# Top-k attention and a gated MLP on one core: the order of a pair of slots, and the merge of two sorted lists

## The chip, the cores and the metric

The kernel runs on one core of a Trainium2 chip. The time is device time in microseconds (us) of one execution. The kernel before has a median of 1507.23 us over 3 runs (1506.77 to 1514.11). Lines L1 and on are lines of the kernel before; PE is TensorE's matrix product, PEld its load of stationary weights, DVE VectorE, ACT ScalarE, POOL GpSimd, SP the engine whose queue issues nearly all DMAs.

## The reference

```python
# q, k, v: (8, 8, 576, 64); w_in: (512, 2048); w_out: (2048, 512); all float32
scores = scale * np.matmul(q, k.transpose(0, 1, 3, 2))
kth = np.partition(scores, -32, axis=-1)[..., -32:-31]
scores = np.where(scores >= kth, scores, -1000000000.0)
attn = np.exp(scores - np.max(scores, axis=-1, keepdims=True))
attn = attn / (np.sum(attn, axis=-1, keepdims=True) + 1e-09)
x = np.matmul(attn, v)              # heads put side by side: (4608, 512)
h = x @ w_in
g = h * (1.0 / (1.0 + np.exp(-1.702 * h)))
out = g @ w_out
```

Each row of scores has 576 entries; the 32 largest are kept, the rest get no weight. The attention's result is the input of a two-layer MLP with a sigmoid gate.

## The kernel before, in words

**Slots.** The attention is cut into 144 slots, 18 per batch. A slot is 128 query rows of one pair of heads (or 64 + 64 rows of two pairs of heads, for the ends of the rows). For a slot n the steps are: `scores` (PE, L282, into PSUM), `copy_scores` (ACT, L294, to the tile `sc` in SBUF), the search for the 32nd largest value (DVE), `bounds` (POOL, L368, two tiny instructions), `exponentials` (ACT: two Prelu, L388, and two Exp with their sums, L391), `split` (ACT, L462: the 16-bit halves of each word are put apart, then a DMA L464 writes them to memory as `rows`), `turn_by_dma` (SP, L470: a transposing DMA brings them back as `pt`), `values` (PE, L530), and the product with the inverse sums, which gives a piece of x (`x_of`, POOL, L544). The inverse sums are made by `invert` (DVE L421 and L423, then a widening copy on POOL, L425) and turned by PE (`sum_rows`, L519).

**The search.** From slot 12 on, the 576 scores of a row are halved: DVE takes the larger of each of 288 pairs (`greater`, L323), POOL makes the smaller ones with two integer instructions (the sum, L326, then the sum less the greater, L327; `lesser`). DVE then finds the 32 largest of `greater` with four rounds of MAX8 (L337) and three of MATCH_REPLACE8 (L340), and the 16 largest of `lesser` with two and one. The lists are sorted. `merge` (L344, one TENSOR_TENSOR with a reversed second input) takes the larger of the k-th of one and the (17-k)-th of the other, and `bound` (L347) reduces these to the cut. `find(n)` issues all of that for slot n, and in its middle `pair_up(n + 1)`.

**The MLP.** Work on 128 tokens is cut into four units. A unit is `hidden` (PE, L580, 32 matmul instructions), `tanh` (ACT, L597 and a copy L600), `gate` (POOL, L609 and L610) and `project` (PE, L628, 8 instructions). Lists in the program (`ready`, `to_gate`, `gated`, `to_project`) hand the units on; a step whose list is empty is left out. When a tile of tokens is done, `leave` (ACT, L634) and a DMA (L636) write it out.

**q and k.** From batch 1 on they are fetched by `load_both` (six DMAs on SP, L184 and L187, into one buffer), then `prepare_by_dma` puts halves apart (ACT, L240, tile `halves`), writes them (SP, L244 to L249) and leaves a transposing DMA (L253) for the list `turns`. FETCH and READY (L657 to L661) say how many slots before a batch each of its four pairs of heads is fetched and prepared; READY's offsets are even, so that `prepare_by_dma` falls into the first half of a pair of slots.

**The order.** It is written out by hand: each engine and each DMA queue runs its instructions in the order in which the program issues them. Slots 0 to 11 run singly (`slot`), with another search and transpositions on PE; they also round the weights. From slot 12 on `two_slots(n)` runs a pair of slots, n even (L842 to L921). On PE a pair before is: hidden, projection, row sums, scores n+2, values n-3 and n-2, scores n+3, hidden, projection. `last_slot` works off the MLP units left over at the end.

**Buffers that matter.** Scores of a slot fill four PSUM banks in two tiles (`ps_s`, 2 buffers), so scores of the next slot wait for the copy of the ones before. The hidden of the second half shares two PSUM buffers with the tile `o` of row sums and values. `pt` has 2 buffers, `sc` 4.

Of the kernel before, what the change touches and what calls it, by code (L numbers as in the profile page):

```python
# [9 lines left out]
ALU = mybir.AluOpType  # L10
ENG = mybir.EngineType
F32 = mybir.dt.float32
U32 = mybir.dt.uint32
I32 = mybir.dt.int32
# [4 lines left out]
P = 128  # L19
TOPK = 32  # L20
LOWEST = -3.4028234663852886e38
# [9 lines left out]
def kernel(  # L31
# [27 lines left out]
    nc = tc.nc  # L59
# [255 lines left out]

    greater, lesser = {}, {}

    def pair_up(n):

        sc = st[n]["sc"]  # L320
        a, b = sc[:, :, 0:HALF], sc[:, :, HALF:S]
        greater[n] = lefts.tile([P, 2, HALF], F32, name="greater", tag="left")
        nc.vector.tensor_tensor(out=greater[n][:], in0=a, in1=b, op=ALU.max)  # L323
        lesser[n] = raws.tile([P, 2, HALF], F32, name="lesser", tag="raw")
        whole = lesser[n][:].bitcast(I32)
        nc.gpsimd.tensor_tensor(out=whole, in0=a.bitcast(I32), in1=b.bitcast(I32), op=ALU.add)  # L326
        nc.gpsimd.tensor_tensor(out=whole, in0=whole, in1=greater[n][:].bitcast(I32), op=ALU.subtract)  # L327

    def topk_of_pairs(n):

        top = st[n]["top"] = small.tile([P, 2, TOPK + TOPK // 2], F32, name="top2", tag="top")
        cut = st[n]["cut"] = small.tile([P, 2], F32, name="cut")
        first, few = greater.pop(n), lesser.pop(n)
        left = lefts.tile([P, 2, HALF], F32, name="left2", tag="left")

        def largest(src, r, i):
            nc.vector.max(top[:, i, 8 * r : 8 * r + 8], src[:, i, :])  # L337

        def remove(to, src, r, i):
            nc.vector.match_replace(to[:, i, :], top[:, i, 8 * r : 8 * r + 8], src[:, i, :], LOWEST)  # L340

        def merge():
            rest = top[:, :, TOPK // 2 : TOPK]
            nc.vector.tensor_tensor(out=rest, in0=rest, in1=top[:, :, : TOPK - 1 : -1], op=ALU.max)  # L344

        def bound():
            nc.vector.tensor_reduce(  # L347
                out=cut[:], in_=top[:, :, TOPK // 2 - 1 : TOPK], axis=mybir.AxisListType.X, op=ALU.min, negate=True
            )

        ops = []
        for r in range(TOPK // 8):
            ops += [lambda r=r, i=i: largest(left if r else first, r, i) for i in range(2)]
            if r < TOPK // 8 - 1:
                ops += [lambda r=r, i=i: remove(left, left if r else first, r, i) for i in range(2)]
        ops += [lambda: pair_up(n + 1) if n + 1 < N else None]
        for r in range(TOPK // 8, TOPK * 3 // 16):
            ops += [lambda r=r, i=i: largest(few, r, i) for i in range(2)]
            if r == TOPK // 8:
                ops += [lambda r=r, i=i: remove(few, few, r, i) for i in range(2)]  # L360
        return ops + [merge, bound]

    def lows(n):

        top, cut = st[n]["top"], st[n]["cut"]
        low = st[n]["low"] = small.tile([P, 2], F32, name="low")
        for i in range(2):
            nc.gpsimd.tensor_scalar(  # L368
                low[:, i : i + 1], cut[:, i : i + 1], top[:, i, 0:1], -1.0, op0=ALU.add, op1=ALU.mult
            )  # L370

    def bounds(n):
# [23 lines left out]
    def divide(n):  # L396

        some = small.tile([P, 2], F32, name="some", tag="sums")
        nc.vector.tensor_scalar_add(some[:], st[n]["den"], 1e-9)
        rden = small.tile([P, 2], F32, name="rden", tag="inverse")  # L400
        nc.vector.reciprocal(rden[:], some[:])
        by = st[n]["by"] = xtt.tile([P, 2, P], F32, name="by", tag="xT_t")
        for i in range(2):
            nc.gpsimd.tensor_scalar(by[:, i, :], ident[:], rden[:, i : i + 1], None, op0=ALU.mult)

    sums = {}

    def sums_of(n):

        k = (n + 1) // 2  # L410
        if k not in sums:
            sums[k] = small.tile([P, 2, 2], F32, name="sums")
        return sums[k][:, (n + 1) % 2, :]

    def invert(n):

        k = (n + 1) // 2
        if k in sums:
            count = 2 if 2 * k < N else 1
            total = sums[k][:, 0:count, :]  # L420
            nc.vector.tensor_scalar_add(total, total, 1e-9)  # L421
            inverse = small.tile([P, 2 * count], F32, name="inverse")
            nc.vector.reciprocal(inverse[:], total.rearrange("p s j -> p (s j)"))  # L423
            wide = sums[k] = raws.tile([P, 2, 2, D], F32, name="wide", tag="raw")
            nc.gpsimd.tensor_copy(  # L425
                out=wide[:, 0:count, :, :].rearrange("p s j d -> p (s j) d"),
                in_=inverse[:].unsqueeze(2).to_broadcast([P, 2 * count, D]),
            )

    def turn(n, first, blocks):  # L430
        pr = st[n]["pr"]
# [84 lines left out]

    def sum_rows(m, to):

        nc.tensor.transpose(to, sums[(m + 1) // 2][:, (m + 1) % 2, :, :], ident[:])  # L519

    def values_at(m, o):

# [121 lines left out]
    def leave_all():  # L644
        while leaving:
            leaving.pop(0)()
# [8 lines left out]


    READY = (-12, -10, -4, -2)  # L657
    READY_1 = (-7, -4, -3, -2)
    FETCH = (-16, -11, -8, -3)
    FETCH_1 = (-12, -6, -3, -2)  # L660
    VALUES = (-1, 1, 1, 3)  # L661
    by_slot = dict(enumerate([2, 2, 3, 3, 3, 3, 3, 3, 3, 3, 2, 2]))
    for n in by_slot:
        first = sum(map(len, list(by_slot.values())[:n]))
# [87 lines left out]
    def bring_all():  # L752

        waiting = len(ready)
        while put_off:
            put_off.pop(0)()
        if len(ready) > waiting:
            hidden()
# [75 lines left out]
    def last_slot():  # L834
# [4 lines left out]
        if may_project(0):  # L839
            project()  # L840

    def two_slots(n):  # L842

        first, second = [later.pop(m, []) for m in (n, n + 1)]
        live = lambda m: 0 <= m < N
        aside = n < N

        def begin(todo):
            for fn, args in todo:
                if fn is not prepare_by_dma:  # L850
                    fn(*args)

        def prepare_some(todo):
            for fn, args in todo:
                if fn is prepare_by_dma:
                    fn(*args)

        def find(m):
            for i, op in enumerate(topk_of_pairs(m) if live(m) else [lambda: None] * 23):
                op()  # L860
                if i == 8 and m % 2 == 0:
                    invert(m - 2)
                if i > 1 and unfinished:
                    finish_one()

        def project_one():
            if may_project(0):
                project(True)

        def measure(m):  # L870
            if live(m):
                bounds(m)
            gate(aside)

        begin(first)
        measure(n - 1)
        if live(n - 1):
            exponentials(n - 1)
            split(n - 1)
        bring_all()  # L880
        find(n)
        hidden()
        project_one()
        tanh(aside)
        prepare_some(first)
        held = [m for m in (n - 3, n - 2) if live(m) and "rows" in st[m]]
        o = ps_t.tile([P, 2, 2, P], F32, name="o", tag="tp") if held else None
        for i, m in enumerate(held):
            sum_rows(m, o[:, i, 0, :])
        if live(n + 2):  # L890
            scores(n + 2)
            copy_scores(n + 2)
        leave_all()
        for i, m in enumerate(held):
            values_at(m, o[:, i, 1, :])
        if live(n - 1):
            turn_by_dma(n - 1)
        while turns:
            turns.pop(0)()
        if live(n + 3):  # L900
            scores(n + 3)
        begin(second)
        measure(n)
        if live(n):
            exponentials(n)
        if held:
            x = raws.tile([P, 2, 2, P], F32, name="x", tag="raw")
            nc.scalar.copy(out=x[:, 0 : len(held)], in_=o[:, 0 : len(held)])
            for i, m in enumerate(held):
                x_of(m, x[:, i, 1, :], x[:, i, 0, :])  # L910
        if live(n):
            split(n)
            turn_by_dma(n)
        hidden(ps_t)
        if live(n + 3):
            copy_scores(n + 3)
        tanh(aside)
        prepare_some(second)
        project_one()
        leave_all()  # L920
        find(n + 1)  # L921

    with tc.manual_schedule():
        opening()
        for n in range(SETTLED + 1):
            slot(n)
        pair_up(SETTLED + 1)
        for n in range(SETTLED + 1, N + 4, 2):
            two_slots(n)
        while ready or to_gate or gated or to_project:  # L930
            last_slot()
# [30 lines left out]
```

## Time and profile before

| what | value |
|---|---|
| median of the runs | 1507.23 us |
| the profiled execution's own time | 1512.53 us |
| its span in the profile | 1510.7 us |
| granted TensorE clock over the span | 0.983 |
| busy PE / PEld / DVE / ACT / POOL | 1443.9 / 1052.8 / 1378.1 / 1171.7 / 891.1 us |
| hidden L580 on PE | 489.6 us in 4096 recorded instructions |
| projection L628 on PE | 518.5 us in 1152 |
| merge L344 on DVE | 132 times, 484 ns mean |
| bound L347 on DVE | 132 times, 190 ns mean |
| `by` L404 on POOL | 22 times, 605 ns mean |
| transposition of pt, L470 | 133 issues, 4.7 us to landing (median) |
| transposition of q and k, L253 | 28 issues, 4.9 us to landing (median) |

The span is the profiled execution from its first to its last instruction. A line of the waits names who waited, for whom, and then the total in us, the number of times and the longest. A line of the timeline gives the start in us from the span's start, the duration, the engine, the line and the operation; consecutive instructions of one kind are merged (x8). Some matmul records are missing from a trace, so a hole in PE's line can be a missing record; L580 has 4608 instructions in the program.

### The profile page before, as it was taken

How to read it: one execution, taken by the hardware profiler on the slowest of the kernel's cores; microseconds unless marked ns; L12 is line 12 of the kernel's file. 1: busy time of each engine (PE TensorE's matmuls, PEld its weight loads, DVE VectorE, ACT ScalarE, POOL GpSimd, SP SyncE). 2: the span in 40 equal slices, each digit the busy share in tenths (PEclk: the TensorE clock that was granted, in tenths of full speed). 3: DMA queues.
4: the chain of work that ended last, by engine and by line, in shares of the span. 5: the costliest groups of instructions: out<-in, count | busy, mean ns of one | idle time of the engine just before them, and what ended most of it. 6: DMA issues, size and time to landing. Idle time of an engine off the chain costs nothing. (4 is left out here: it accounts for less than half of the span.)

```text
span 1510.7 us, 31439 instructions
## 1 busy us (share of the span) xinstructions
PE 1443.9 (96%) x10729; PEld 1052.8 (70%) x10729; DVE 1378.1 (91%) x4542; ACT 1171.7 (78%) x1846; POOL 891.1 (59%) x1117
## 2 busy tenths in 40 slices
PE   6789878999999999999999999999999999999998
PEld 5667555767777777767777767777777777777775
DVE  7999989999999999999999999999999999999800
ACT  6998878878878787888878787888878888777720
POOL 3788645666666666666666556666666666656500
PEclk7899989999999999999999999999999999999999
DMA  7451876766858587666767667585776767444520
GB/s 226 134 156 43 196 198 184 190 174 171 188 158 211 149 201 194 159 182 157 210 160 182 167 178 191 159 199 150 196 194 155 192 161 207 140 129 134 133 55 14
DMA packets 533777, 248.35 MB, mean 164 GB/s; under 512 B 465136, under 2 KB 507888, under 8 KB 533616
## 3 DMA queue, kind: packets, MB, share of 16 engines
q1 hardware_dynamic: 533184, 246.05, 62.1%
q8 instruction: 84, 1.38, 0.4%
q14 instruction: 77, 0.63, 0.1%
q10 hardware_dynamic: 432, 0.30, 0.1%
HBM read 45.09 MB, written 105.32 MB: 100 GB/s over the span
## 5 line engine op out<-in xcount | busy, mean ns | idle before, releaser
L580 PEld LDWEIGHTS ph<-xT,win 128*128 128x128 f32 x4096 | 474.3, 192 | 69.7 <-issue 53.7
L628 PE MATMUL po<-wout,th 128*128 128x512 f32 x1152 | 518.5, 593 | 1.5 <-POOL wout L147 1.5
L580 PE MATMUL ph<-xT,win 128*128 128x128 f32 x4096 | 489.6, 277 | 12.0 <-POOL xT L544 12.0
L628 PEld LDWEIGHTS po<-wout,th 128*128 128x128 f32 x1152 | 208.1, 191 | 211.1 <-issue 207.9
L337 DVE MAX8 top<-left 128x8 f32<-128x288 f32 x792 | 325.6, 446 | 0.0
L462 ACT COPY sc<-pr 128x2304 uint16<-128x2304 uint16 x133 | 281.5, 2117 | 2.2
L294 ACT ACTIVATE sc<-s_ps 128x576 f32<-128x576 f32 x288 | 172.0, 653 | 128.9 <-PE s_ps L282 126.7
L544 POOL TENSOR_TENSOR xT<-x 128x128 f32<-128x128 f32 x117 | 51.4, 457 | 332.4 <-DVE top L344 161.3
L340 DVE MATCH_REPLACE8 left<-top,left 128x288 f32<-128x288 f32 x528 | 229.7, 443 | 0.0
L391 ACT ACTIVATE pr<-sc,low 128x576 f32<-128x576 f32 x288 | 220.9, 777 | 0.0
L337 DVE MAX8 top<-lesser 128x8 f32<-128x288 f32 x528 | 214.2, 447 | 0.0
L388 ACT ACTIVATE sc<-sc,cut 128x576 f32<-128x576 f32 x288 | 208.7, 783 | 1.6 <-DVE cut L347 1.3
L327 POOL TENSOR_TENSOR lesser<-lesser,greater 128x576 int32<-128x576 int32 x132 | 186.0, 1409 | 22.2 <-DVE greater L323 12.7
L282 PE MATMUL s_ps<-qk_t 64*128 64x288 f32 (+1 forms) x1280 | 186.3, 437 | 9.8 <-ACT sc L294 9.1
L326 POOL TENSOR_TENSOR lesser<-sc 128x576 int32<-128x576 int32 x132 | 187.5, 1421 | 0.0
L610 POOL TENSOR_TENSOR th<-th,h 128x512 f32<-128x512 f32 x127 | 161.7, 1273 | 10.6
L530 PE MATMUL o<-pt,v_l 128*64 128x128 f32 (+1 forms) x2384 | 146.2, 266 | 10.5 <-DMA pt<-rows 10.4
L530 PEld LDWEIGHTS o<-pt,v_l 128*64 128x64 f32 x2384 | 121.1, 138 | 38.6 <-issue 24.9
L597 ACT ACTIVATE th<-ph 128x512 f32<-128x512 f32 x144 | 86.5, 601 | 73.2 <-PE ph L580 73.0
L323 DVE TENSOR_TENSOR greater<-sc 128x576 f32<-128x576 f32 x132 | 104.4, 791 | 36.7 <-ACT sc L294 28.5
L282 PEld LDWEIGHTS s_ps<-qk_t 64*128 64x128 f32 (+1 forms) x1280 | 101.5, 180 | 51.3 <-issue 21.6
L609 POOL TENSOR_SCALAR th<-th 128x512 f32<-128x512 f32 x127 | 78.8, 620 | 66.2 <-ACT th L597 66.0
(86 smaller groups left out, 1648.0 us busy)
## 6 DMA issues: line engine op xcount, KB each, us to landing
rows<-sc SPq DMA_DIRECT2D x133, 576.0 KB, 3.2
qk_rows<-halves SPq DMA_DIRECT2D x56, 256.0 KB, 2.9
qk_l<-in_q_dram SPq DMA_DIRECT2D x64, 128.0 KB, 2.9
raw<-in_moe_w_in_dram SPq DMA_DIRECT2D x16, 512.0 KB, 5.1
v_l<-in_v_dram SPq DMA_DIRECT2D x32, 256.0 KB, 3.0
raw<-in_moe_w_out_dram SPq DMA_DIRECT2D x16, 512.0 KB, 3.7
out_dram<-ob SPq DMA_DIRECT2D x32, 256.0 KB, 2.9
qk_l<-in_k_dram SPq DMA_DIRECT2D x62, 128.0 KB, 2.9
```

The costliest lines, as they stand in the source:

```text
L282: nc.tensor.matmul(ps[i][rows, c, 0:HALF], lhsT=qT[b, hps[p]][on, cols], rhs=kT[b, hps[p]][on, FIRST[i] + c * HALF : FIRST[i] + (c + 1) * ...
L294: nc.scalar.mul(out=to, in_=ps[i][:, :, 0:HALF], mul=SCALE)
L326: nc.gpsimd.tensor_tensor(out=whole, in0=a.bitcast(I32), in1=b.bitcast(I32), op=ALU.add)
L327: nc.gpsimd.tensor_tensor(out=whole, in0=whole, in1=greater[n][:].bitcast(I32), op=ALU.subtract)
L337: nc.vector.max(top[:, i, 8 * r : 8 * r + 8], src[:, i, :])
L340: nc.vector.match_replace(to[:, i, :], top[:, i, 8 * r : 8 * r + 8], src[:, i, :], LOWEST)
L388: nc.scalar.activation(sc[:, i, :], sc[:, i, :], AF.Prelu, bias=cut[:, i : i + 1], alpha=HUGE)
L391: nc.scalar.activation(pr[:, i * S : (i + 1) * S], sc[:, i, :], AF.Exp, bias=low[:, i : i + 1], accum_out=den[:, i : i + 1],)
L462: nc.scalar.copy(out=halves, in_=pr[:].bitcast(U16).rearrange("p (k h) -> p h k", h=2))
L530: nc.tensor.matmul(o[j * D : (j + 1) * D, cols], lhsT=main[:, j, c, :] if c < NF else tail[:, j, :], rhs=pt[:, MAIN[j] + c if c < NF else ...
L580: nc.tensor.matmul(ph[:, i * tiles * P : (i + 1) * tiles * P], lhsT=win[:, c, f * P : (f + 1) * P], rhs=xT[c], start=(c == 0), stop=(c == ...
L628: nc.tensor.matmul(po[:], lhsT=gT[:, i * P : (i + 1) * P], rhs=wout[:, f, :], start=(f == 0), stop=(f == FC - 1))
```

## The change

Four things change.

1. The order of a pair. On PE it becomes: projection, hidden, hidden, projection, row sums, scores n+3, values n-2 and n-1, scores n+4. The first scores of a pair (n+2) have been issued at the end of the pair before. On ACT the copy of scores n+2 stands ahead of `find(n)`, the second `tanh` ahead of `split(n)`, the copy of scores n+3 and the copy of x after `find(n + 1)`. `invert` is issued in `find(n)` after its 16th operation and takes the sums of n-2 and n-1. `turn_by_dma(n)` stands at the end of the pair. The loop has one pair fewer.
2. `pair_up` is split: `sum_pairs` (POOL, the sum) right after the scores are copied, `part_pairs` (DVE's maximum, POOL's difference) where `pair_up` stood.
3. The merge: MAX8 writes the second list in falling order of address (a negative step) into the tile `top`, which grows from 48 to 64 words a row; one TENSOR_REDUCE over pairs of places takes the maxima.
4. Offsets: READY_1, FETCH_1 and VALUES, and `by` on POOL gets a second operation (times 1.0).

```diff
+    def sum_pairs(n):
+        a, b = halves_of(n)
+        lesser[n] = raws.tile([P, 2, HALF], F32, name="lesser", tag="raw")
+        nc.gpsimd.tensor_tensor(
+            out=lesser[n][:].bitcast(I32), in0=a.bitcast(I32), in1=b.bitcast(I32), op=ALU.add
+        )
+
+    def part_pairs(n):
+        a, b = halves_of(n)
         greater[n] = lefts.tile([P, 2, HALF], F32, name="greater", tag="left")
         nc.vector.tensor_tensor(out=greater[n][:], in0=a, in1=b, op=ALU.max)
-        lesser[n] = raws.tile([P, 2, HALF], F32, name="lesser", tag="raw")
         whole = lesser[n][:].bitcast(I32)
-        nc.gpsimd.tensor_tensor(out=whole, in0=a.bitcast(I32), in1=b.bitcast(I32), op=ALU.add)
         nc.gpsimd.tensor_tensor(out=whole, in0=whole, in1=greater[n][:].bitcast(I32), op=ALU.subtract)
...
         def merge():
-            rest = top[:, :, TOPK // 2 : TOPK]
-            nc.vector.tensor_tensor(out=rest, in0=rest, in1=top[:, :, : TOPK - 1 : -1], op=ALU.max)
+            both = top[:, :, 0:TOPK].rearrange("p i (s k) -> p i k s", s=2)
+            nc.vector.tensor_reduce(
+                out=top[:, :, TOPK + TOPK // 2 :], in_=both, axis=mybir.AxisListType.X, op=ALU.max
+            )
...
-            nc.gpsimd.tensor_scalar(by[:, i, :], ident[:], rden[:, i : i + 1], None, op0=ALU.mult)
+            nc.gpsimd.tensor_scalar(by[:, i, :], ident[:], rden[:, i : i + 1], 1.0, op0=ALU.mult, op1=ALU.mult)
...
-    READY_1 = (-7, -4, -3, -2)
+    READY_1 = (-7, -6, -4, -2)
     FETCH = (-16, -11, -8, -3)
-    FETCH_1 = (-12, -6, -3, -2)
-    VALUES = (-1, 1, 1, 3)
+    FETCH_1 = (-12, -6, -5, -3)
+    VALUES = (0, 1, 2, 3)
...
+    def bring_x(held, o):
+        x = raws.tile([P, 2, 2, P], F32, name="x", tag="raw")
+        nc.scalar.copy(out=x[:, 0 : len(held)], in_=o[:, 0 : len(held)])
+        for i, m in enumerate(held):
+            x_of(m, x[:, i, 1, :], x[:, i, 0, :])
...
+        held = [m for m in (n - 2, n - 1) if live(m) and m >= SETTLED]
...
-                if i == 8 and m % 2 == 0:
-                    invert(m - 2)
+                if i == 15 and m == n and held:
+                    invert(held[0], held[-1])
...
         begin(first)
-        measure(n - 1)
         if live(n - 1):
+            bounds(n - 1)
             exponentials(n - 1)
             split(n - 1)
         bring_all()
+        if live(n + 2):
+            copy_scores(n + 2)
         find(n)
+        if live(n + 2):
+            sum_pairs(n + 2)
+        project_one()
         hidden()
-        project_one()
+        leave_all()
         tanh(aside)
         prepare_some(first)
...
+        gate(aside)
         if live(n - 1):
             turn_by_dma(n - 1)
         while turns:
             turns.pop(0)()
+        begin(second)
+        if live(n):
+            bounds(n)
+            exponentials(n)
+        hidden(ps_t)
+        tanh(aside)
+        gate(aside)
+        if live(n):
+            split(n)
+        find(n + 1)
+        project_one()
+        leave_all()
+        o = ps_t.tile([P, 2, 2, P], F32, name="o", tag="tp") if held else None
+        for i, m in enumerate(held):
+            sum_rows(m, o[:, i, 0, :])
         if live(n + 3):
             scores(n + 3)
+            copy_scores(n + 3)
+            sum_pairs(n + 3)
+        for i, m in enumerate(held):
+            values_at(m, o[:, i, 1, :])
+        if held:
+            bring_x(held, o)
         if live(n):
             turn_by_dma(n)
+        if live(n + 4):
+            scores(n + 4)
         prepare_some(second)
...
-        pair_up(SETTLED + 1)
-        for n in range(SETTLED + 1, N + 4, 2):
+        for n in range(SETTLED + 1, SETTLED + 3):
+            sum_pairs(n)
+        part_pairs(SETTLED + 1)
+        scores(SETTLED + 3)
+        for n in range(SETTLED + 1, N + 2, 2):
             two_slots(n)
```

More of the change, by code (lines that the diff above doesn't have):

```diff
@@ L316, with halves_of @@
     greater, lesser = {}, {}
-    def pair_up(n):
+    def halves_of(n):
         sc = st[n]["sc"]
-        a, b = sc[:, :, 0:HALF], sc[:, :, HALF:S]
+        return sc[:, :, 0:HALF], sc[:, :, HALF:S]
+    def sum_pairs(n):
[6 more added lines that the diff above has]
+        a, b = halves_of(n)
         greater[n] = lefts.tile([P, 2, HALF], F32, name="greater", tag="left")
         nc.vector.tensor_tensor(out=greater[n][:], in0=a, in1=b, op=ALU.max)
-        lesser[n] = raws.tile([P, 2, HALF], F32, name="lesser", tag="raw")
         whole = lesser[n][:].bitcast(I32)
-        nc.gpsimd.tensor_tensor(out=whole, in0=a.bitcast(I32), in1=b.bitcast(I32), op=ALU.add)
         nc.gpsimd.tensor_tensor(out=whole, in0=whole, in1=greater[n][:].bitcast(I32), op=ALU.subtract)
     def topk_of_pairs(n):
-        top = st[n]["top"] = small.tile([P, 2, TOPK + TOPK // 2], F32, name="top2", tag="top")
+        top = st[n]["top"] = small.tile([P, 2, 2 * TOPK], F32, name="top2", tag="top")
         cut = st[n]["cut"] = small.tile([P, 2], F32, name="cut")
@@ L334, in topk_of_pairs, with found @@
         left = lefts.tile([P, 2, HALF], F32, name="left2", tag="left")
+        def found(r, i, written=False):
+            if r < TOPK // 8:
+                at = (8 * r + TOPK) % (TOPK + TOPK // 2)
+                return top[:, i, at : at + 8]
+            end = 2 * TOPK - 8 * (r - TOPK // 8) - TOPK
+            return top[:, i, end - 1 : end - 9 : -1] if written else top[:, i, end - 8 : end]
         def largest(src, r, i):
-            nc.vector.max(top[:, i, 8 * r : 8 * r + 8], src[:, i, :])
+            nc.vector.max(found(r, i, True), src[:, i, :])
         def remove(to, src, r, i):
-            nc.vector.match_replace(to[:, i, :], top[:, i, 8 * r : 8 * r + 8], src[:, i, :], LOWEST)
+            nc.vector.match_replace(to[:, i, :], found(r, i), src[:, i, :], LOWEST)
         def merge():
-            rest = top[:, :, TOPK // 2 : TOPK]
-            nc.vector.tensor_tensor(out=rest, in0=rest, in1=top[:, :, : TOPK - 1 : -1], op=ALU.max)
+            both = top[:, :, 0:TOPK].rearrange("p i (s k) -> p i k s", s=2)
+            nc.vector.tensor_reduce(
+                out=top[:, :, TOPK + TOPK // 2 :], in_=both, axis=mybir.AxisListType.X, op=ALU.max
+            )
         def bound():
             nc.vector.tensor_reduce(
-                out=cut[:], in_=top[:, :, TOPK // 2 - 1 : TOPK], axis=mybir.AxisListType.X, op=ALU.min, negate=True
+                out=cut[:], in_=top[:, :, TOPK + TOPK // 2 - 1 :], axis=mybir.AxisListType.X, op=ALU.min, negate=True
             )
@@ L355, in topk_of_pairs @@
                 ops += [lambda r=r, i=i: remove(left, left if r else first, r, i) for i in range(2)]
-        ops += [lambda: pair_up(n + 1) if n + 1 < N else None]
+        ops += [lambda: part_pairs(n + 1) if n + 1 < N else None]
         for r in range(TOPK // 8, TOPK * 3 // 16):
@@ L368, in lows @@
             nc.gpsimd.tensor_scalar(
-                low[:, i : i + 1], cut[:, i : i + 1], top[:, i, 0:1], -1.0, op0=ALU.add, op1=ALU.mult
+                low[:, i : i + 1], cut[:, i : i + 1], top[:, i, TOPK : TOPK + 1], -1.0, op0=ALU.add, op1=ALU.mult
             )
@@ L403, in divide, with invert @@
         for i in range(2):
-            nc.gpsimd.tensor_scalar(by[:, i, :], ident[:], rden[:, i : i + 1], None, op0=ALU.mult)
+            nc.gpsimd.tensor_scalar(by[:, i, :], ident[:], rden[:, i : i + 1], 1.0, op0=ALU.mult, op1=ALU.mult)
     sums = {}
     def sums_of(n):
-        k = (n + 1) // 2
+        k = n // 2
         if k not in sums:
             sums[k] = small.tile([P, 2, 2], F32, name="sums")
[L413 to L428, printed above, removed]
+        return sums[k][:, n % 2, :]
+    def invert(first, last):
+        k = first // 2
+        on = slice(first % 2, last % 2 + 1)
+        count = last + 1 - first
+        total = sums[k][:, on, :]
+        nc.vector.tensor_scalar_add(total, total, 1e-9)
+        inverse = small.tile([P, 2 * count], F32, name="inverse")
+        nc.vector.reciprocal(inverse[:], total.rearrange("p s j -> p (s j)"))
+        wide = sums[k] = raws.tile([P, 2, 2, D], F32, name="wide", tag="raw")
+        nc.gpsimd.tensor_copy(
+            out=wide[:, on, :, :].rearrange("p s j d -> p (s j) d"),
+            in_=inverse[:].unsqueeze(2).to_broadcast([P, 2 * count, D]),
+        )
     def turn(n, first, blocks):
@@ L517, in sum_rows @@
     def sum_rows(m, to):
-        nc.tensor.transpose(to, sums[(m + 1) // 2][:, (m + 1) % 2, :, :], ident[:])
+        nc.tensor.transpose(to, sums[m // 2][:, m % 2, :, :], ident[:])
     def values_at(m, o):
@@ L868, in project_one @@
                 project(True)
[L870 to L873, printed above, removed]
         begin(first)
-        measure(n - 1)
         if live(n - 1):
+            bounds(n - 1)
             exponentials(n - 1)
@@ L880, in two_slots @@
         bring_all()
+        if live(n + 2):
+            copy_scores(n + 2)
         find(n)
+        if live(n + 2):
+            sum_pairs(n + 2)
+        project_one()
         hidden()
-        project_one()
+        leave_all()
         tanh(aside)
         prepare_some(first)
[L886 to L895, printed above, removed]
+        gate(aside)
         if live(n - 1):
@@ L899, in two_slots @@
             turns.pop(0)()
+        begin(second)
[13 more added lines that the diff above has]
+            sum_rows(m, o[:, i, 0, :])
         if live(n + 3):
             scores(n + 3)
-        begin(second)
-        measure(n)
-        if live(n):
[L905 to L912, printed above, removed]
+            copy_scores(n + 3)
[4 more added lines that the diff above has]
+            bring_x(held, o)
+        if live(n):
             turn_by_dma(n)
[L914 to L917, printed above, removed]
+        if live(n + 4):
+            scores(n + 4)
         prepare_some(second)
-        project_one()
-        leave_all()
-        find(n + 1)
     with tc.manual_schedule():
```

## The prediction

> **What bounds the kernel now.** I read the page's busy shares first, then busy time by stretch, the waits of PE and DVE between 300 and 1440 us, and the timeline of one pair of slots.
>
> ```profile
> PE 1443.9 (96%) x10729; PEld 1052.8 (70%) x10729; DVE 1378.1 (91%) x4542; ACT 1171.7 (78%) x1846; POOL 891.1 (59%) x1117
> ...
> 200.00:220.00 20.00, 14.02 (x81) 11.08 (x82) 13.19 (x43) 16.02 (x23) 9.42 (x12) 0.76 0.82 203
> 240.00:260.00 20.00, 17.34 (x130) 13.38 (x130) 19.83 (x65) 14.30 (x24) 10.31 (x14) 0.91 0.69 187
> 400.00:420.00 20.00, 20.00 (x147) 14.37 (x143) 19.56 (x69) 15.98 (x27) 12.08 (x15) 1.00 0.89 192
> 1440.00:1511.00 71.00, 66.81 (x399) 46.76 (x397) 6.44 (x11) 7.64 (x14) 1.61 (x4) 0.99 0.10 25
> ```
>
> Columns after the length of the stretch: busy PE, PEld, DVE, ACT, POOL, then granted clock. Up to about 280 us VectorE is full and PE has holes; from there PE is full (20.00 of 20.00) with VectorE a little below; the last 70 us are MLP alone. The waits between 300 and 1440 us say how little PE stands still:
>
> ```profile
> PE ph L580 <- POOL xT L544: 10.3, 14, 0.8
> PE o L530 <- DMA pt<-rows: 4.3, 3, 2.8
> ...
> DVE greater L323 <- ACT sc L294: 21.6, 39, 2.7
> ```
>
> One pair on PE, first column the start:
>
> ```profile
> 801.67 0.38 PE L519 MATMUL o<-ident,wide 128*128 128x128 f32 x2
> 801.98 1.24 PE L282 MATMUL s_ps<-qk_t 64*128 64x288 f32 x8
> 803.15 1.09 PE L530 MATMUL o<-pt,v_l 128*64 128x128 f32 x16
> 804.08 0.39 PE L530 MATMUL o<-pt,v_e 128*64 128x128 f32 x4
> 804.29 1.04 PE L530 MATMUL o<-pt,v_l 128*64 128x128 f32 x16
> 805.17 0.39 PE L530 MATMUL o<-pt,v_e 128*64 128x128 f32 x4
> 805.49 1.24 PE L282 MATMUL s_ps<-qk_t 64*128 64x288 f32 x8
> 806.66 3.84 PE L580 MATMUL ph<-xT,win 128*128 128x128 f32 x32
> 810.33 3.60 PE L628 MATMUL po<-wout,th 128*128 128x512 f32 x8
> 813.77 3.73 PE L580 MATMUL ph<-xT,win 128*128 128x128 f32 x32
> ```
>
> Start to start: row sums 0.31, scores 1.17, values 1.14 and 1.20, scores 1.17, hidden 3.67 (3.57 after a projection), projection 3.44, hidden 3.57, projection 3.43. From one L519 to the next that is 19.1 us, and most pairs after 280 us last just that: nothing but a hole on PE can be saved or added there.
>
> **The change, part by part.** Times are against the profiled execution, 1512.5 us (span 1510.7), which is 5.3 us over the median of the three runs, 1507.2.
>
> *The new order on PE, pairs with a copy of q and k.* In a new pair PE runs projection, hidden, hidden, projection, row sums, scores, values n-2, values n-1, scores. The values of n-1 used to wait for the next pair; now they are due in the pair in which their exponentials are made. Let 0 be the start of the first projection. PE reaches values n-1 at 3.44 + 3.57 + 3.57 + 3.44 + 0.31 + 1.17 + 1.14 = 16.6 us. The transposition that feeds it (L470) stands on SP behind the writes of `prepare_by_dma` (L244 to L249) in pairs that have one, and these wait on ACT for `halves` (L240), which stands behind the tanh of the first hidden:
>
> ```profile
> 800.35 0.59 ACT L597 ACTIVATE th<-ph 128x512 f32<-128x512 f32 x1
> 801.30 2.12 ACT L240 COPY halves<-qk_l 128x2304 uint16<-128x2304 uint16 x1
> 803.45 0.94 SPq L244 DMA_DIRECT2D qk_rows<-halves  x2
> 805.80 2.64 SPq L470 DMA_TRANSPOSE pt<-rows  x1
> ...
> DMA to landing us min/median/max: 6.3/6.3/6.3
> ```
>
> That line is this one transposition's landing. The first hidden ends at 3.44 + 3.73 = 7.17; tanh to `halves` 0.95; `halves` to L244 2.15: 10.3. From L244 to landing, over the 24 such pairs after 280 us, the trace gives 7.4 to 10.2, mean 8.4 (here 2.35 + 6.3). So it lands at 18.7 and PE waits 18.7 - 16.6 = 2.1 us. Four of nine pairs have such a copy: 24 x 2.1 = **+50**, bounds 24 x 1.1 = +26 and 24 x 3.9 = +94. Before, the same landing had until the next pair; that is the cover which is gone. In pairs without a copy the same chain is: exponentials from -0.6 (behind the copy of x), 3.2, split 2.05, rows landed 3.8 after issue, transposition 4.7: 13.2, so 3.4 us early. A pair that fetches q and k in its first half (six loads, 3.8 us of SP each time) just behind a copy pair lands at about 17: **+2** over six such pairs, bounds 0 and +6.
>
> A rule that speaks against this: the Trainium skill, TensorE: Matmul & The Clock Gate, part on the clock gate, has the clock halved after an idle window of about 3.4 us. The trace agrees: after a hole of 3.57 us at 239 the clock shows 0.91 in that stretch, after one of 2.84 us at 901 nothing. By that page only the longest of my waits (3.9 us) would cost more, an estimated 2 us in all.
>
> *Holes that go.* The hidden of the second half stood right behind the multiplication by `wide` (POOL L544). Now x is made at a pair's end and a 3.4 us projection stands between. After 280 us, 15 pairs last 20.1 instead of 19.1 for this: **-15** (bounds -15 and -10.3, the bare waits). Late transpositions and the few other long pairs there (19.5, 19.6, 20.5, 22.2): **-5** (bounds 0 and -5). What is late next is the transposition above.
>
> *The first pairs, 148 to 280 us.* PE's holes are 1.48, 0.73, 2.90, 0.95, 8.41, 0.84, 3.57, 1.47: 20.4 us, plus some 5 at a low clock. The 8.41 come from q/k loads issued in the half that copies them (ACT idle 5.04 before L240); the new FETCH_1 asks for the last one half a pair sooner, so that goes. But hp 1 of batch 1 is now copied in pair 12, whose loads are issued at 154.7 to 158.6: copy about 161, writes 163 to 166, transposition of slot 11 landed about 172, against PE ready near 163.5: a new hole of 8.5, then some 4, 2 and 4 in the next three pairs while SP catches up. Net **-5**, from the slow clock and VectorE's share below; bounds -20 (all holes gone) and +10.
>
> *Merge by TENSOR_REDUCE.* L344 takes 191 ns when alone and 484 in the mean (up to 1282): at 817.06 it lasts 0.82, until POOL's L327 ends. A reduction of 64 elements stands nearest to L347 (68 elements, 187 to 193 ns, never longer): 0.29 x 132 = 39 us of VectorE. After 280 us VectorE has 1 us a pair to spare, so **0**; ten slots before that are in the -5 above; bounds 0 and -3.
> The Trainium skill, VectorE: DVE Perf Modes, rules for kernel authors, calls tensor_reduce the slowest DVE op, to be restructured. By the 151 + N cycles which that page gives for fp32, an estimate would be 0.22 us here: the sum stays as it is, since the row is as short as the tensor_tensor alone.
>
> *Waits added on VectorE.* `invert` now stands in find(n) behind the sums of n-1: exponentials end at 2.6, VectorE is there about then, 17.9 of work against 19.1: **0**, bounds 0 and +1 a pair (that is a rival). Behind it queue the second lists and `cut`.
> *ACT.* The copy of scores n+2 moves ahead of find(n) and stands behind split(n-1): done at 5.7, before the tanh can start at 7.2. The second half ends with the copy of scores n+3 at 17.2 even with a copy of q and k, and PE reaches scores n+4 at 17.8: 0, bounds 0 and +0.6 in 24 pairs. The value loads stay on SP a half pair from where they were, 1.7 us of issue where SP is idle: 0.
> *POOL.* `sum_pairs` moves ahead of `part_pairs`, same instructions; `lows`, x and the gates keep order with 1 us to spare before the projection: 0, bounds 0 and +6. `by` with two operations: L404 takes 605 ns for 128 elements, L609 with two takes 620 for 512; VectorE hides it (59.68 of 60 us busy from 100 to 160): 0, bounds -6 (PE's waits for it) and 0.
> *MLP units side by side, one pair of slots less at the end.* Same matmuls, hidden behind hidden as behind a projection: 0, bounds +-6 (0.1 a pair).
>
> Sum: 50 + 2 - 15 - 5 - 5 = +27, 1539.5 of 1512.5; on the median **1534**.
>
> **The rivals.**
> 1. *The wait does not open* (faster). L244 to landing would have to fall to 6.3. For it: the shortest landing of any pt is 4.4 and the shortest way to the issue 2.3, 6.7 together, and traffic at that point of the pair is thinner. Against: the least of 24 sums is 7.4. Then -23 to -25: 1484. It decides the sign where the mean wait falls under 1 us.
> 2. *It opens by half*, 1 us, the low bound: 26 + 2 - 25 = +3, 1510: no change that can be told.
> 3. *VectorE becomes the bound through `invert`*: exponentials behind x, x behind late values, 1 us in each of 60 pairs on top: 1594. Against: VectorE's 1.2 us to spare a pair.
> 4. *The merge stays at 484 ns* (the new instruction also held up by POOL): time unchanged, PE sets it.
>
> **How the numbers follow.** Forecast 0.60 (its own range 1510 to 1558: waits of 1.1 to 3.1 us); rival 1 0.18; rival 2 0.16; rival 3 0.06; rival 4 goes with any of them. Range 1488 to 1558: it leaves out about half of rival 1, and rival 3. A measurement tells 0.5%, 7.5 us, from no change: faster 0.20 (rival 1 and the edge of 2), same 0.15, slower 0.65.
>
> **What the profile after would show.** Right: PE waits at the value matmuls for "DMA pt<-rows", about 2 us, some 24 times, none of PE's hidden on POOL xT; pairs of 19.1 and 21.2; the merge near 0.19. Wrong: no such waits, or holes before projections (POOL th) or scores (ACT sc), which would mean ACT's or POOL's order binds, or VectorE idle before the sums.

## The result, and the profile after

The changed kernel is slower by 1.7%: 1534.82 us (median of 4 runs, 1533.66 to 1537.04) against 1509.2 us for the kernel before in the same comparisons (median of 4). The ratio is 1.0167, 95% interval 1.0136 to 1.0199. The profiled execution took 1537.04 us, its span is 1535.3 us, 24.6 us over the span before.

The busy shares of the page, the merge's row, and PE's waits between 300 and 1450 us (who waited for whom, total us, times, longest):

```profile
PE 1450.6 (94%) x10729; PEld 1054.3 (69%) x10729; DVE 1348.8 (88%) x4540; ACT 1184.6 (77%) x1847; POOL 886.6 (58%) x1121
...
L361 DVE TENSOR_REDUCE top<-top x132: 219/221/225, 158.2 to 1467.3; 128x32 f32<-128x64 f32 x132
...
PE o L549 <- DMA pt<-rows: 35.5, 26, 2.5
PE po L647 <- POOL th L629: 0.6, 1, 0.6
```

VectorE has 29 us less to do and the kernel is 25 us longer. The holes before hidden (10.3 us) are gone; in their place PE waits 26 times for `pt`. One such pair on PE (line numbers of the changed kernel: L549 values, L599 hidden, L647 projection, L538 row sums), which starts at 818.94:

```profile
818.94 3.70 PE L647 MATMUL po<-wout,th 128*128 128x512 f32 x8
822.48 7.31 PE L599 MATMUL ph<-xT,win 128*128 128x128 f32 x64
829.63 3.60 PE L647 MATMUL po<-wout,th 128*128 128x512 f32 x8
833.06 0.38 PE L538 MATMUL o<-ident,wide 128*128 128x128 f32 x2
833.37 1.24 PE L282 MATMUL s_ps<-qk_t 64*128 64x288 f32 x8
834.54 1.09 PE L549 MATMUL o<-pt,v_l 128*64 128x128 f32 x16
835.47 0.39 PE L549 MATMUL o<-pt,v_e 128*64 128x128 f32 x4
837.25 1.09 PE L549 MATMUL o<-pt,v_l 128*64 128x128 f32 x16 [1.39 <-DMA pt<-rows]
```

And the chain that ends this wait, on ACT and SP:

```profile
826.25 0.60 ACT L616 ACTIVATE th<-ph 128x512 f32<-128x512 f32 x1 [1.52 <-PE ph L599]
826.75 0.58 ACT L619 COPY h<-ph 128x512 f32<-128x512 f32 x1
827.21 2.13 ACT L240 COPY halves<-qk_l 128x2304 uint16<-128x2304 uint16 x1
...
829.36 0.93 SPq L244 DMA_DIRECT2D qk_rows<-halves  x2
830.34 0.57 SPq L248 DMA_DIRECT2D qk_rows<-halves  x1
830.95 1.40 SPq L249 DMA_DIRECT2D qk_rows<-halves  x1
832.46 2.53 SPq L489 DMA_TRANSPOSE pt<-rows  x1
...
DMA to landing us min/median/max: 4.7/4.7/4.7
```

From the pair's start the tanh begins at 7.3, the copy at 8.3, the first write at 10.4, the transposition at 13.5, and it lands 4.7 later, at 18.2. PE had come at 16.7 (835.68, 1.14 us after the first values; the wait of 1.39 us is counted from the end of their last instruction, 0.18 later). The last line of the view is this transposition alone.

How much longer than 19.11 us the pairs with n = 24 to 138 are, counted from one L538 to the next, by what they do (for the kernel before from one L519 to the next):

| pairs | before | after | e1 | e10 | e8 |
|---|---|---|---|---|---|
| the 24 with a q/k copy | 11.8 | 44.0 | 17.1 | 28.6 | 7.8 |
| the 6 behind the first two copies of a batch (fetch q and k) | 2.7 | 5.5 | 32.7 | 3.7 | 13.3 |
| the 6 behind the last two copies | 0.0 | 0.0 | 14.3 | 0.0 | 0.7 |
| the 22 others | 4.9 | -0.1 | 9.3 | 1.1 | 0.7 |
| all, us | 19.4 | 49.4 | 73.4 | 33.3 | 22.5 |

(e1, e10 and e8 are experiments below.) The pairs account for +30.0 us (49.4 less 19.4), nearly all of it in those with a copy; the start and the end give 5.4 back, which makes the 24.6.

### The profile page after: what moved, and what is told of

Its sections match the earlier page's. It is cut to its first block, busy times and chain, and to the rows that moved or that the text cites. A ratio compares the mean times of both kernels' runs of the same rounds, so it can differ in the third digit from the quotient of the medians.

```text
span 1535.3 us, 31220 instructions
## 1 busy us (share of the span) xinstructions
PE 1450.6 (94%) x10729; PEld 1054.3 (69%) x10729; DVE 1348.8 (88%) x4540; ACT 1184.6 (77%) x1847; POOL 886.6 (58%) x1121
## 4 chain that ended last, share of the span: by engine, by line
PE 78%; DMA 11%; ACT 4%; SPq 3%; DVE 2%; issue 1%; POOL 0%; ACTq 0%; POOLq 0%
PE ph L599 30%; PE po L647 29%; DMA pt<-rows 10%; PE o L549 8%; PE s_ps L282 8%; ACT halves L240 1%; DVE top L304 1%; SPq L184 1%; PE tp L459 1%; DMA rows<-sc 1%; DVE left L307 1%; ACT sc L294 1%; PE o L538 1%; PE none L169 1%; SPq L244 1%
## 5 line engine op out<-in xcount | busy, mean ns | idle before, releaser
L647 PE MATMUL po<-wout,th 128*128 128x512 f32 x1152 | 528.1, 601 | 3.4 <-POOL wout L147 2.1
L599 PEld LDWEIGHTS ph<-xT,win 128*128 128x128 f32 x4096 | 468.0, 192 | 32.3 <-issue 30.7
L599 PE MATMUL ph<-xT,win 128*128 128x128 f32 x4096 | 469.4, 275 | 0.1
L647 PEld LDWEIGHTS po<-wout,th 128*128 128x128 f32 x1152 | 208.6, 191 | 242.1 <-issue 233.3
L354 DVE MAX8 top<-left 128x8 f32<-128x288 f32 x792 | 320.9, 446 | 0.0
L354 DVE MAX8 top<-lesser 128x8 f32<-128x288 f32 x528 | 218.9, 446 | 0.0
L549 PE MATMUL o<-pt,v_l 128*64 128x128 f32 (+1 forms) x2384 | 149.3, 269 | 50.3 <-DMA pt<-rows 50.3
L549 PEld LDWEIGHTS o<-pt,v_l 128*64 128x64 f32 x2384 | 121.3, 138 | 83.0 <-DMA pt<-rows 57.5
L629 POOL TENSOR_TENSOR th<-th,h 128x512 f32<-128x512 f32 x129 | 165.4, 1283 | 11.4 <-POOL th L628 1.0
L864 ACT COPY x<-o 128x512 f32<-128x512 f32 (+1 forms) x67 | 39.0, 583 | 128.3 <-PE o L549 128.3
L440 DVE TENSOR_SCALAR sums<-sums 128x4 f32<-128x4 f32 (+1 forms) x67 | 29.0, 432 | 105.3 <-ACT pr L410 105.3
```

Source lines behind the costliest of these rows:

```text
L354: nc.vector.max(found(r, i, True), src[:, i, :])
L549: nc.tensor.matmul(o[j * D : (j + 1) * D, cols], lhsT=main[:, j, c, :] if c < NF else tail[:, j, :], rhs=pt[:, MAIN[j] + c if c < NF else ...
L599: nc.tensor.matmul(ph[:, i * tiles * P : (i + 1) * tiles * P], lhsT=win[:, c, f * P : (f + 1) * P], rhs=xT[c], start=(c == 0), stop=(c == ...
L647: nc.tensor.matmul(po[:], lhsT=gT[:, i * P : (i + 1) * P], rhs=wout[:, f, :], start=(f == 0), stop=(f == FC - 1))
```

## The experiments

Ratios are to the kernel before, timed on the same chip; the kernel before took 1509.2, 1515.9, 1516.6 and 1515.3 us in the four comparisons, so kernels are compared by their ratios. The theory is the forecast's: values n-1 wait for a transposition that stands behind the copy of q and k.

| run | what differs from the changed kernel | PE's waits for pt after 300 us | ratio (95%) |
|---|---|---|---|
| after | nothing | 35.5 us, 26 times | 1.0167 (1.0136 to 1.0199) |
| e1 | transposition of n-1 ahead of the q/k writes | 43.0, 20 | 1.0321 (1.0288 to 1.0355) |
| e10 | rows(n) ahead of the q/k transposition and loads | 23.3, 25 | 0.9990 (0.9977 to 1.0003) |
| e8 | both | 17.1, 15 | 0.9945 (0.9930 to 0.9960) |
| e9 | both, and the first loads behind rows(n-1) | 15.9, 16 | 0.9941 (0.9918 to 0.9964) |
| e5 | the copy of q/k made earlier on ACT and SP | 9.9, 12 | 0.9992 (0.9980 to 1.0005) |
| e2 | the copy made twice | 83.2, 24 | one run: 1634.95 us |
| e4 | sums inverted five instructions later | 37.7, 25 | one run: 1545.1 us |
| e6 | the two hiddens apart | 0 | 1.2213 (1.2193 to 1.2234) |
| e3 | (kernel before with the new merge) | 6.4, 6 | 1.0002 (0.9982 to 1.0021) |

### e1: the transposition ahead of the writes

```diff
         tanh(aside)
-        prepare_some(first)
         gate(aside)
         if live(n - 1):
             turn_by_dma(n - 1)
+        prepare_some(first)
```

> The changed kernel, with the transposition of slot n-1 issued on SP ahead of the four writes of the q/k copy; no other queue or engine changes its order. Theory (the wait of the values of n-1 for pt, in pairs with a q/k copy, is what made the kernel slower): the transposition is issued at about 8.5 us of the pair and lands at 13 to 14, PE comes at 16.6, so the waits of PE for pt after 300 us (35.5 us in 26 places) go, with what they cost around them; the pairs after 290 us are all near 19.1; 1535 falls to 1483 to 1492, under the kernel before. Rival (VectorE's wait for the sums, 105 us in the trace, sets the time): 1535, unchanged within 5 us, since VectorE's order is the same.

Measured: 1563.79 us, by the ratios 1.5% more than the changed kernel, where 43 to 52 us less (3%) were expected. The copy's own pairs did get shorter (44.0 to 17.1 us in the table), but the pairs behind them are now 56.3 us too long, where it was 5.4. SP shows why (timeline of SP from a copy's pair into the next, which fetches q and k; L253 is the transposition of q and k, L483 the write of `rows`, L489 the transposition of `pt`, L184 and L187 the loads):

```profile
496.50 2.63 SPq L253 DMA_TRANSPOSE qk_t<-qk_rows  x1
499.17 0.58 SPq L483 DMA_DIRECT2D rows<-sc  x1
503.03 2.78 SPq L489 DMA_TRANSPOSE pt<-rows  x1
505.86 1.27 SPq L184 DMA_DIRECT2D qk_l<-in_q_dram  x2
507.17 0.63 SPq L187 DMA_DIRECT2D qk_l<-in_q_dram  x1
507.84 1.28 SPq L184 DMA_DIRECT2D qk_l<-in_k_dram  x2
509.16 0.63 SPq L187 DMA_DIRECT2D qk_l<-in_k_dram  x1
509.84 0.59 SPq L483 DMA_DIRECT2D rows<-sc  x1
513.05 2.70 SPq L489 DMA_TRANSPOSE pt<-rows  x1
```

The transposition of q and k must wait for its rows to land; before, the transposition of n-1 had filled that wait. Now SP stands still (45.3 us over the kernel for this), rows(n), whose words ACT had ready at 493.1, goes out at 499.17, and what stands behind it is late too. The next pair's rows(n-1), ready at 500.6, goes out at 509.84; its `pt` costs PE a wait of 3.88 us that ends at 517.9. In the changed kernel PE waits 1.15 us in the copy's pair and 2.44 us in this one; here it is 0.90 us (a projection behind its gate) and 3.88. The theory in its first form (the wait belongs to the one chain) does not stand. A second form: SP's queue is in order and three of its issues in a pair block until something has landed, so the order decides which ready work is locked in behind a blocked wait, and the cost may appear a pair later.

### e8: rows(n) before whatever can block, and e10: that half alone

In e8 e1's edit stays, and the transposition of q/k and the loads of the second half move behind split(n):

```diff
-        while turns:
-            turns.pop(0)()
-        begin(second)
         if live(n):
             bounds(n)
...
             split(n)
+        while turns:
+            turns.pop(0)()
+        begin(second)
         find(n + 1)
```

> As e1_turn_first (transposition of n-1 ahead of the writes of q/k), and the transposition of q/k and the second half's loads are issued on SP only after the writing of rows(n). In e1 SP stood still 45 us for the written q/k rows before that transposition, with rows(n) queued behind it, and the pair after paid up to 4 us. Theory (SP's queue is a chain of blocked waits; a wait must be filled with work that is ready): rows(n) goes out at 16 to 17 us of the pair, the wait for the q/k rows is filled, the waits for pt after 300 us fall below 12 us in all; ratio 0.983 to 0.995 to the kernel before. Rival (any order on SP only moves the wait): waits of 30 us or more in other pairs, ratio above 1.01.

> The changed kernel with the second half of e8's edit alone: the transposition of q/k and the second half's loads behind the writing of rows(n), but the writes of q/k still ahead of the transposition of n-1. Theory: in pairs with a q/k copy the transposition of n-1 still ends at about 18.7 us of the pair, so the waits for pt after 300 us stay at 25 to 45 us, and only what was handed on to later pairs goes: ratio 1.005 to 1.017. With e1 (the other half alone, 1.0321) and e8 (both, 0.9945) this says whether the two halves add: if the order of rows(n) alone were the cause, this run would be as fast as e8.

```profile
PE o L549 <- DMA pt<-rows: 17.1, 15, 3.0
...
PE o L549 <- DMA pt<-rows: 23.3, 25, 2.0
```

The lines are PE's waits after 300 us of e8 and of e10. e8 measured 0.9945, 0.55% faster than the kernel before and 2.2% faster than the changed one, with the waits at 17.1 and not under 12; e10 measured 0.9990, below the range I gave. So the two halves do not add: one alone costs 1.5% (e1), the other alone gains 1.8% (e10), both gain 2.2%. The place of rows(n) is the larger part. e10 also shortens the copy's own pairs (44.0 to 28.6). With it goes a faster landing of the 24 transpositions of n-1 behind q/k writes after 285 us: from issue to landing they take 5.28 us in the changed kernel and 4.85 in e10, where the transposition of q/k and the loads are not issued right behind them. That the DMAs issued right behind are what slows the landing is likely, but no run has it alone. PE, VectorE, ACT and POOL have the same instructions in the same order in the changed kernel, e1, e8 and e10.

### e9: the loads at a pair's start

```diff
-        begin(first)
         if live(n - 1):
...
             split(n - 1)
+        begin(first)
```

> As e8_rows_first, and the loads that a pair issues at its start stand behind the writing of rows(n-1) on SP. What e8 still waits for pt (17.1 us after 300 us, the longest 2.95 and 3.04) lies mostly in pairs that fetch q and k first: at 318.6 to 322.5 six loads stand ahead of rows(n-1), though its words were ready. Theory (SP's queue must hold ready work in its blocked waits): the waits for pt after 300 us fall below 7 us, ratio 0.980 to 0.993 to the kernel before. Rival (these waits come from the landing of the transposition itself): 15 us or more stay, ratio as e8, 0.993 to 0.996.

Measured 0.9941, and 15.9 us of waits: the rival's numbers. In pairs that fetch q and k the excess fell from 13.3 to 8.3 us, other pairs took it up (the pairs that fetch the next batch's first q and k: 0.9 to 3.6). What is left is not in the place of these loads; it was not pursued.

### e5: the copy earlier, e2: the copy twice

```diff
             copy_scores(n + 2)
+        prepare_some(first)
         find(n)
...
         tanh(aside)
-        prepare_some(first)
         gate(aside)
```

> The changed kernel, with the whole prepare_by_dma (copy of q/k on ACT, its writes on SP) issued ahead of find(n), so that ACT makes the copy right after the scores of n+2, at about 5.7 to 7.8 us of the pair and not at 8.2 to 10.3; SP keeps the order writes, transposition of n-1, transposition of q/k, loads. Theory (values n-1 wait for the chain tanh, copy, writes, transposition, and SP's queue hands every delay on): that chain ends 2.4 us sooner, the waits for pt after 300 us (35.5 us) fall below 12 us, nothing on SP comes later than in the changed kernel, so no later pair pays: 25 to 45 us under the changed kernel, a ratio of 0.985 to 1.000 to the kernel before. Rival (the copy only displaces tanh and gates on ACT and POOL): ratio 1.01 or more.

```diff
         nc.scalar.copy(out=halves[:], in_=words.rearrange("p c (e h) -> p c h e", h=2))
+        nc.scalar.copy(out=halves[:], in_=words.rearrange("p c (e h) -> p c h e", h=2))
```

> The changed kernel, with the copy of q/k into halves done twice on ACT (2.1 us more in the 28 such copies); the output is the same. Theory: each of the 24 to 26 late transpositions lands 2.1 us later, and PE's waits for pt grow by some 50 us after 300 us, to 85 to 90; the clock may fall behind more of them; 1535 grows to 1580 to 1630. Rival (ACT has room: the copy is hidden, the waits come from the queue of DMAs alone): under 10 us more.

PE's waits after 300 us, first e5, then e2 (whose values stand on L550):

```profile
PE o L549 <- DMA pt<-rows: 9.9, 12, 2.8
PE po L647 <- POOL th L629: 6.6, 10, 1.6
...
PE o L550 <- DMA pt<-rows: 83.2, 24, 4.5
```

Both as the theory has them. With the copy 3.0 us sooner in its pair (mean start 11.1 us after the pair's row sums, before 14.1; 2.4 had been expected) the waits fall to 9.9 us and the kernel is as fast as the one before; some of the gain goes into projections that now wait for a later gate. With the copy twice, 2.1 us longer, the waits in the 24 pairs grow from 33.3 to 83.2 us, 2.1 each. The other half of e2's 98 us (between the spans of the profiled executions) is the clock: granted 0.950 over the span against 0.982, which is at most (0.050 x 1633) - (0.018 x 1535) = 54 us of lost cycles; during some of them PE stood still anyway. The rival, that ACT hides the copy, is out.

### e4: the sums later, e3: the merge alone

```diff
-                if i == 15 and m == n and held:
+                if i == 20 and m == n and held:
```

> The changed kernel, with invert (the addition and the reciprocal on VectorE) issued after the last MAX8 of the second list in place of the first, five instructions (about 2 us) later in find(n). Theory: VectorE's wait for the sums (105 us in all) falls below 30 us, the time stays at 1535 within 5 us, as PE waits for pt and not for VectorE. Rival (VectorE's wait sets the time): 1535 falls by 20 us or more.

The time did not fall (1545.1 us in a single run; the kernel before showed 1515.9 on that chip, so 1.019), and PE's waits for pt are the same 37.7 us. So VectorE's wait for the sums doesn't set the time. But I had that wait wrong: it fell from 105.3 to 75.6 us in all, not below 30. VectorE has time to spare in each pair, and much of it still collects at this wait.

In e3 the kernel before gets the new merge alone (the tile `top` of 64 words, the reversed MAX8 output, TENSOR_REDUCE).

> The kernel before, with the merge by TENSOR_REDUCE alone. Theory: the merge falls from 484 to about 190 ns (39 us of VectorE busy time), but PE sets the time from 280 us on, so the whole is 0 to 5 us faster than the kernel before, 1502 to 1509. Rival A: VectorE bounds, 20 us or more faster. Rival B: the reduction is held up as the TENSOR_TENSOR was, and stays near 480 ns.

Row of the merge in e3, then VectorE's wait between 300 and 1440 us:

```profile
L351 DVE TENSOR_REDUCE top<-top x132: 220/221/225, 157.7 to 1433.4; 128x32 f32<-128x64 f32 x132
...
DVE greater L323 <- ACT sc L294: 58.4, 55, 5.1
```

The merge is 221 ns instead of 484, 35 us less of VectorE, and the time is the same (1.0002). The wait of `greater` for the scores was 21.6 us before and is 58.4 now, 36.8 us more: the gain came out as waiting.

### e6: the hiddens apart

```diff
+        project_one()
         hidden(ps_t)
+        leave_all()
         tanh(aside)
...
         find(n + 1)
-        project_one()
-        leave_all()
```

> The changed kernel, with the second projection moved between the two hiddens on PE, so that the MLP units no longer stand side by side. Theory: PE does the same work and reaches the values at the same 16.6 us, so side by side is worth nothing on PE itself; but the second tanh can start only at 14.1 instead of 10.6, split(n) and the copy of scores n+3 follow it on ACT and end at about 18.1, and PE comes to scores n+4 at 17.8: up to 0.3 us in pairs without a late pt, 0 to 20 us in all, ratio 1.015 to 1.030. Rival (hidden behind hidden saves PE time): the pairs last 19.3 or more without any wait, and row by row the hidden takes longer than 3.57 us.

Measured 1.2213, far outside. PE between 813 and 826 us, and what it waited for, on POOL:

```profile
813.75 3.70 PE L647 MATMUL po<-wout,th 128*128 128x512 f32 x8
817.28 3.73 PE L599 MATMUL ph<-xT,win 128*128 128x128 f32 x32
824.02 2.47 PE L647 MATMUL po<-wout,th 128*128 128x512 f32 x3 [3.01 <-POOL th L629]
...
822.00 0.61 POOL L628 TENSOR_SCALAR th<-th 128x512 f32<-128x512 f32 x1
822.70 1.27 POOL L629 TENSOR_TENSOR th<-th,h 128x512 f32<-128x512 f32 x1
```

The second projection takes the unit whose hidden has just ended, so tanh and gate (1.0 and 1.9 us) lie open: 182.7 us of such waits in 61 pairs. After most of these holes of 3 us the clock is halved too (0.911 over the span): at most 0.089 x 1852 - 0.018 x 1535 = 137 us. The waits for `pt`, 35.5 us in the changed kernel, are gone, so 182.7 - 35.5 + 137 = 284 of the 317 us over the changed kernel have a name; the rest is open. So the second hidden beside the first does nothing for PE, and is the cover of the gate; I had taken the projection to have an older unit to work on.

## The prediction, point by point

**The direction and the mechanism** were right: forecast 1534, measured 1534.8. That the total comes out to 1 us is in part luck: errors of -6, +3.5 and others in the terms cancel, and within the largest term a wait that was taken too long is made up for by costs that the sum put at nothing. The sum by its terms, against the profiled span:

- *Wait of values n-1, +50*: mechanism right, term too large by 6. Its chain was forecast as 7.2, 8.2, 10.3 us and shows as 7.3, 8.3, 10.4. From the first write to the landing I took the 8.4 us of the kernel before; the changed kernel needs 2.55 + 5.28 = 7.8. Part of the difference: in 6 of the 24 pairs of the kernel before the first write stood directly behind another DMA on SP (3.4 to 3.8 us from there to the issue of the transposition), in the changed kernel in none. So the waits in the 24 pairs are 33.3 us, 1.4 each and not 2.1; the pairs are 44.0 us longer. The other 10.7 us are the clock in two of these pairs (1.8 us each, below) and 0.2 to 0.6 us around each wait, such as the 0.18 us in the view above. The sum had neither; the clock stood beside it with an estimated 2 us in all.
- *Pairs that fetch q and k behind a copy, +2*: 5.5, of which one pair makes 4.2 (a wait of 2.44 us and the clock behind it).
- *Holes before hidden and others, -20*: right; the 19.4 us of these pairs before are gone, no hidden waits for x.
- *The first pairs, -5*: right with luck. With the end of the kernel, which the pairs' count does not separate from it, it came to -5.4 (24.6 less 30.0). The new hole in pair 12 is there, 5.25 us instead of 8.5, then 1.75, 2.05 and 4.71 in the next three pairs, where I had 4, 2 and 4.
- *Merge, 0*: right, and shown by e3. It takes 221 ns; the row I had put beside it (190 ns) is a little short. The 0.22 us worked out from the Trainium skill, VectorE: DVE Perf Modes, came closer, though the page gives its 151 + N for a tensor_tensor add. The same page's advice against tensor_reduce (rules for kernel authors) cost nothing to leave aside here: alone, the two-input instruction is the shorter one (191 ns), but in the mean it took 484. All 62 of the 132 that took over 230 ns began while a POOL instruction ran and ended with it; the 132 reductions took 219 to 225 ns.
- *`invert`, 0*: right (e4, a single run), though VectorE waits longer there than I said.
- *Side by side, 0*: right for the changed kernel, wrong in its reason. I compared hidden behind hidden with hidden behind a projection, and not what stands between a hidden and the projection of the same unit (e6).

**The cover.** "Before, the same landing had until the next pair; that is the cover which is gone" holds. What the prediction lacks is the queue behind the transposition. I looked for what SP must do before it, and not for what SP must do after it; so my first remedy, e1, made things worse.

**The rivals.** The wait opened, so 1 is out; its least sum from write to landing was 7.2, not 6.3. Rival 2 was nearer than the time says: the bare wait of 1.4 us lies closer to its 1.0 than to the forecast's 2.1, and the 0.45 us a pair around the wait (the clock included) bring the time near the forecast. VectorE did not become the bound (3), the merge did get shorter (4). The offsets of batch 1 and `by`, which act ahead of the pairs counted above, were not run alone.

## What to carry to other kernels

An in-order DMA queue with issues that block until something has landed is a chain of its own: when one step is moved on it, write out the whole queue over two periods, put work that is ready ahead of what blocks, and look for the cost one period later. Where one engine is full over the whole period, only the holes on that engine count; time saved elsewhere comes out as waiting, and the place of that waiting says nothing about what sets the time. A step that seems to bring nothing to its own engine can be the cover of another engine's latency, so ask for each neighbour what it hides before it is moved.

## What the runs showed of the hardware

The clock falls after shorter holes than I had taken. Stretches (length, busy PE, PEld, DVE, ACT, POOL, then granted clock) around a hole of 2.44 us and one of 2.49 us in the changed kernel, and around one of 2.84 us in the kernel before:

```profile
512.00:520.00 8.00, 5.56 (x44) 4.00 (x41) 4.68 (x16) 3.25 (x7) 3.27 (x6) 0.79 0.65 176
1115.00:1123.00 8.00, 5.51 (x40) 3.21 (x37) 5.12 (x18) 4.51 (x10) 4.88 (x7) 0.79 0.86 209
...
900.00:910.00 10.00, 7.16 (x99) 6.29 (x98) 9.81 (x36) 7.71 (x12) 3.57 (x5) 1.00 0.89 234
```

A clock of 0.79 over 8 us is half the clock for 3.4 us: (1 - 0.79) x 8 / 0.5. It came after holes of 2.44, 1.95 and 2.49 us (from 512.7, 675.9 and 1115.5) and not after 2.84. So a hole below the 3.4 us of the Trainium skill, TensorE: Matmul & The Clock Gate (part on the clock gate), can halve the clock, and one of the same size need not.

What tells them apart shows in the starts of the low stretches: within a run they lie a whole number of steps of 3.413 us apart (in the changed kernel 515.34, 679.18 and 1119.49, so 48 and 129 steps). Here are the step with the hole of 2.44 us and the next one, then a step with 1.87 us of idle time and its next (busy PE alone, then granted clock):

```profile
511.93:515.34 3.41, 0.97 (x20) 1.00 0.80 253
515.34:518.75 3.41, 3.41 (x26) 0.50 0.28 62
...
856.67:860.08 3.41, 1.54 (x26) 1.00 1.27 271
860.08:863.49 3.41, 3.41 (x22) 1.00 0.39 154
```

Over the traces of all eleven kernels, after 280 us, each step at full clock in which PE was idle for 2.0 us or more was followed by one at half the clock (96 of 96), and none with less than 1.8 us was (of 3884); of the 13 in between, 7 were. The 2.84 us of the kernel before lie across a mark, 1.12 us on one side and 1.73 on the other.

A POOL instruction with two scalar operations can be shorter than with one: `by` took 603 ns (median) with one and 371 with a second, times 1.0, on the same 128 elements. What it is worth in time was not run alone; the prediction put it at 0, because VectorE was full there.
